# Attention output of four batches as one block of 64x64 matmul tiles in a fused attention and MoE kernel

## The chip, the cores and the metric

The kernel runs on one core of a Trainium2 chip. The metric is the device time of one execution in microseconds, as the median of several runs. The core has five engines that run side by side and wait for one another by semaphores: PE multiplies matrices into PSUM (eight banks), DVE and ACT do elementwise work and empty PSUM, POOL does elementwise work as well, and SP starts most of the DMA transfers.

## The reference

```python
def _attn_ref(q, k, v):                       # 8 batches, 8 heads, 576 rows, 64 columns
    q_s = softmax of q over its 64 columns
    k_s = softmax of k over the 576 rows
    kv  = einsum('bhsd,bhse->bhde', k_s, v)   # one 64x64 matrix per batch and head
    return einsum('bhsd,bhde->bhse', q_s, kv)

def _moe_ref(x, w_in, w_out, beta):           # x: 4608 x 512, the heads side by side
    h = x @ w_in                              # 512 -> 2048
    g = h * (1.0 / (1.0 + exp(-beta * h)))
    return g @ w_out                          # 2048 -> 512
```

(The two softmaxes are written out in the original; here they are shortened.) A batch has 576 rows: 512 make one slab, and the 64 remainder rows of all eight batches make a ninth.

## The kernel before

The program is a list of instructions recorded in order; each engine runs its own in that order, and a helper derives the semaphore waits from which buffers and PSUM banks each instruction reads and writes. The helper gives a PSUM bank one user at a time: an instruction that writes a bank waits until the other engines' earlier accesses to it are done.

Slab t (0 to 8) has a first part, x times `w_in` (64 matmuls of 512 columns), and a second part, g times `w_out`. The second part uses seven products in place of eight by sums and differences of blocks: seven products of 16 matmuls, 112 matmuls of 256 columns, in the fixed order below. PSUM banks `z5` and `z2` are used in turn.

```python
# second part of slab t (cut); one tick of the slot counter per matmul
prod_s(...); prod(z5, *gs2(0), *wo(1, 1), True, ...)   # matmuls 1 to 32
TS = PS[s];  TS = TS - PS[z5]                          # DVE
prod(z2, *gs2(1), *wo(0, 0), True)                     # 33 to 48
TS = TS - PS[z2]                                       # DVE: sets bank z2 free
if t > 3: g_diff(0); g_diff(1)                         # DVE
prod(z5, *gt(0, 0), *wo(0, 1), False); copy(z5, 0, 1, ACTE)    # 49 to 64
prod(z2, *gt(NG, 1), *wo(1, 0), False); copy(z2, 1, 0, ACTE)   # 65 to 80
prod(z5, *gt(0, 1), *wsum(1), False, True); last(z5, 1, 1)     # 81 to 96
prod(z2, *gt(NG, 0), *wsum(2), False, True); last(z2, 0, 0)    # 97 to 112
```

The attention of batch t+1 is placed between these matmuls at given slots (slot 64 is the start of the second part, and each of its matmuls counts 32/56). Two heads share a matmul whose 128x128 weights hold two 64x64 blocks and two blocks of masked zeros:

```python
def kvd(b, hp, bk, c):       # KVD = (K^T V) * 1/sum * MASK, 128x128 with zero corners
    ...
def out_mm(b, hp, bk):
    mm(PS[bk][:, :], KVD[kd(b)][:, hp, :], QT[i][:, hp, :], True, True, ...)
def out_step(b, hp, pool=MB, eng=DVE):     # one matmul and its copy out of PSUM
    ...
def attn(b):
    s = [(24 if b == 5 else 16, steps(kv_all, b))]
    x = []
    for hp in range(NHP):
        x += out_step(b, hp, MB, ACTE if hp % 2 else DVE)
    s += spread(x, 84, 108)
    return s
# and in slabs 4 to 6: eight remainder matmuls of 64 columns (outr_steps), spread too
```

The softmax here doesn't subtract the row's maximum and nothing guards it: scores larger than these inputs give would overflow.

Of the kernel before, what the change touches and what calls it, by code (L numbers as in the profile page):

```python
# [19 lines left out]
NM = DM // 128  # L20
NG = NF // 2
NHP = H // 2
SM = 512
SR = S - SM
NSLAB = 9
# [4 lines left out]


class Op:
    __slots__ = ("eng", "fn", "deps", "slot", "pos", "inc", "count", "clock")

    def __init__(self, eng, fn, slot):
        self.eng, self.fn, self.slot = eng, fn, slot
        self.deps = []
        self.inc = False
        self.count = 0
        self.clock = None  # L40


class Program:
# [46 lines left out]
    def plan(self):  # L90
        for op in self.ops:
            op.deps = [d for d in op.deps if not (d.eng == PE and op.eng == PE and d.slot is None)]
            for d in op.deps:
                d.inc = True
        counts = {}
        for op in self.ops:
            if op.slot is not None:
                key = ("dma", op.slot)
                counts[key] = counts.get(key, 0) + 16
                op.count = (key, counts[key])  # L100
            elif op.inc:
                key = ("eng", op.eng)
                counts[key] = counts.get(key, 0) + 1
                op.count = (key, counts[key])
        known = {}
        waits = []
        for op in self.ops:
            k = known.setdefault(op.eng, {})
            need = {}
            for d in sorted(op.deps, key=lambda d: -d.pos):  # L110
                key, n = d.count
                if k.get(key, 0) >= n:
                    continue
                if need.get(key, 0) < n:
                    need[key] = n
                for kk, nn in d.clock.items():
                    if k.get(kk, 0) < nn:
                        k[kk] = nn
                k[key] = max(k.get(key, 0), n)
            waits.append(sorted(need.items(), key=str))  # L120
            op.clock = dict(k)
            if op.count:
                op.clock[op.count[0]] = op.count[1]
        return counts, waits
# [31 lines left out]
def bass_efficient_attn_shen__then__act_swish_beta_kernel(  # L156
# [12 lines left out]
    with ExitStack() as es:  # L169
# [129 lines left out]
                load_rem("vrf", vt_h, VRF, b)  # L299


        def exp_main(name, srcb, dstb, b, hp0, n):
            i = b % 2
            for hp in range(hp0, hp0 + n):
                o = bass.AP(dstb[i], hp * 512, [[2048, 128], [64, 2], [128, 4], [1, 64]])
                a = bass.AP(srcb[i], hp * 512, [[2048, 128], [256, 2], [64, 4], [1, 64]])
                add(ACTE, lambda e, o=o, a=a: e.activation(o, a, ACT.Exp),  # L307
                    r=[(name + "f", i, hp)], w=[("e" + name, i, hp)])

# [14 lines left out]
                bass.AP(EKS[b], 0, [[512, 128], [1, 512]]), bass.AP(KRF, 0, [[512, 128], [1, 512]]),  # L324
                ACT.Exp), r=[("krf", 0), ("krf", 1)], w=[EKSK[b]])

        def exp_qr():
            add(ACTE, lambda e: e.activation(EQR[:, :, :], QRF[:, :, :], ACT.Exp),
                r=[("qrf", 0), ("qrf", 1)], w=["eqr"])

        def norm_main(b, hp0, n, eng=DVE, sums=True, mult=True):
            i = b % 2
# [21 lines left out]
        def cast_v(b, hp, eng=POOL, after=()):  # L354
            i = b % 2
            o = bass.AP(VB[i], hp * VW, [[4 * NHP * VW, 128], [NHP * VW, 4], [HW, 2], [1, 64]])
            a = bass.AP(VF[i], hp * 512, [[2048, 128], [64, 4], [256, 2], [1, 64]])
            add(eng, lambda e: (e.copy if eng == ACTE else e.tensor_copy)(o, a),  # L358
                r=[("vf", i, hp), ("vone", i)], w=[("vb", i, hp)], after=after)

# [63 lines left out]
        def kd(b):  # L424
            return b if b < 2 else 2 + b % 4

        def tiled(b):
            return b > 3

        def kvd(b, hp, bk, c):  # L430
            i = b % 2
            a = bass.AP(PS[bk], c, [[512, 128], [0 if tiled(b) else HW, 2], [1, D]])
            add(DVE, lambda e: e.scalar_tensor_tensor(
                KVD[kd(b)][:, hp, :].rearrange("p (a b) -> p a b", b=D), a, RC[i][:, hp:hp + 1],
                MASK[:, :].rearrange("p (a b) -> p a b", b=D), ALU.mult, ALU.mult),
                r=[("ps", bk), ("rc", i, hp), "mask0", "mask1", "mask2"], w=[("kvd", kd(b), hp)],
                bank=[bk])

        def kv_steps(b, hps, pool=MB):
            i = b % 2  # L440
            st = {}

            def one(n, hp, j):
                if n == 0 and j == 0:
                    st["b"] = bank(pool)
                bk = st["b"]
                l, r_, ke, kv, ko = kv_rows(b, hp, j)
                if not tiled(b):
                    mm(PS[bk][:, 256 * n:256 * n + VW - 1], l, r_[:, 0:VW - 1], j == 0, j == 4,
                       r=ke + kv, w=[("ps", bk)], bk=bk)  # L450
                for h in range(2) if tiled(b) else ():
                    p = slice(64 * h, 64 * h + 64)
                    add(PE, lambda e, h=h, p=p: e.matmul(  # L453
                        PS[bk][p, 256 * n:256 * n + D + 1], l[:, p], r_[:, HW * h:HW * h + D + 1],
                        start=j == 0, stop=j == 4, tile_position=(0, 64 * h),
                        skip_group_check=True),
                        r=ke + kv, w=[("ps", bk)], bank=[bk])
                if n == len(hps) - 1 and j == 4:
                    c, k_ = hps[0], len(hps)
                    s_ = bass.AP(PS[bk], D, [[512, 128], [256, k_]])  # L460
                    add(DVE, lambda e: e.reciprocal(RC[i][:, c:c + k_], s_),
                        r=[("ps", bk)], w=[("rc", i, h2) for h2 in hps], bank=[bk])
                    for m, h2 in enumerate(hps):
                        kvd(b, h2, bk, 256 * m)
            return [lambda n=n, hp=hp, j=j: one(n, hp, j) for n, hp in enumerate(hps)
                    for j in range(5)]
# [17 lines left out]
        def outr_steps(b):  # L484
# [14 lines left out]
                        w=[("xt8", pi)], bank=[bk])  # L499
            return [lambda hp=hp, e_=e_: one(hp, e_) for hp in range(NHP) for e_ in range(2)]  # L500

        def turn(b, hp0, n):
            i = b % 2
            o = bass.AP(QT[i], hp0 * 512, [[2048, 128], [128, 4 * n], [1, 128]])
            a = bass.AP(EQ[i], hp0 * 512, [[2048, 128], [1, 512 * n]])
            add(SP, lambda e: e.dma_start_transpose(o, a),
                r=[("eq", i, hp) for hp in range(hp0, hp0 + n)],
                w=[("qt", i, hp) for hp in range(hp0, hp0 + n)], slot=f"tq{i}{hp0}")
# [21 lines left out]
            return kv_steps(b, (0, 1)) + kv_steps(b, (2, 3))  # L530

        def attn(b):
            s = [(24 if b == 5 else 16, steps(kv_all, b))]
            x = []
            for hp in range(NHP):
                x += out_step(b, hp, MB, ACTE if hp % 2 else DVE)
            s += spread(x, 84, 108)
            return s

        def attn_late(b):  # L540
            x = []
            for hp in range(NHP):
                x += out_step(b, hp, MB, ACTE if hp % 2 else DVE)
            if b < 4:
                s = spread(kv_steps(b, (0, 1)), 97, 101) + spread(kv_steps(b, (2, 3)), 101, 105)
                s += [(105, lambda: g_diff(1))]
                return s + spread(x[0:2], 117, 120)
            s = [(96, steps(kv_all, b)), (99, lambda: g_diff(1))]
            return s + spread(x, 107, 123)

        def spread(steps, lo, hi):
            return [(lo + (hi - lo) * k / len(steps), s) for k, s in enumerate(steps)]
# [310 lines left out]
        for t in range(NSLAB):  # L863
# [13 lines left out]
            elif t < 4:  # L877
                todo = attn_late(t + 1)
                if t > 1:
                    todo += [(1, steps(out_step, t, 2, MB, ACTE)), (2.5, steps(out_step, t, 3))]  # L880
                if t == 3:
                    todo += [(4, one(norm_turn, 4, 2))]
                if t == 1:
                    todo += [(1, steps(out_step, 1, 2, (3,), ACTE)),
                             (3, steps(kv_steps, 1, (3,), (7,))),
                             (6, steps(out_step, 1, 3, (7,), DVE)),
                             (6.1, one(w_sum, 2, 4, 4)), (6.2, one(w_diff, 0)),
                             (6.3, one(w_diff, 1))]
            elif t < 7:
                todo = attn(t + 1)  # L890
                if t > 3:
                    todo += spread(outr_steps(2 * t - 5), *((72, 88), (72, 88), (60, 76))[t - 4])
            elif t == 7:
                todo = spread(outr_steps(1), 32, 48)
            todo = sorted(todo, key=lambda x: -x[0])
# [90 lines left out]
            elif t == 3:  # L986
# [3 lines left out]
                on(3, g_diff, 0)  # L990
                on(4, norm_turn, 5, 0)
                on(5, norm_turn, 5, 2)
                on(4, exp_qr)
                on(5, exp_k, 5)
                on(5, norm_turn_rem)
                on(5, casts, 5)
# [8 lines left out]
                on(3, norm_turn, b, 0)  # L1005
                on(4, norm_turn, b, 2)
            if 3 < t < 7:
                on(0, exp_qr)
                on(5, norm_turn_rem)
            if t in (4, 5):  # L1010
                on(0, load_rem, "qrf", qt_h, QRF, (6, 0)[t - 4])
# [35 lines left out]
```

## Time and profile before

| | before |
|---|---|
| median | 273.45 us (273.27 to 273.69, 6 runs) |
| PE busy | 97% of the span |
| PE on the chain that ended last | 85% |
| DVE, ACT busy | 71%, 67% |

PE sets the end, so the question for any change is what PE does, and for what PE waits. The lines are shown and read in the prediction. In this document I compare slabs by one length, taken from PE's timeline: from the start of the first matmul of the second part (the one with `WSUM,GS`) to the same matmul one slab later. Two of the lines from which the lengths before are taken (columns: start in us, us, engine and line, operation, out<-in, shape, count):

```profile
174.19 1.04 PE L754 MATMUL PS<-WSUM,GS 128*128 128x256 bf16 x8
202.28 0.60 PE L754 MATMUL PS<-WSUM,GS 128*128 128x256 bf16 x4
```

So slab 5 is 202.28 - 174.19 = 28.09 us long. By the same reading slab 3 is 28.63, slab 4 27.99, slab 6 27.28 and slab 7, whose second part holds no attention, 26.04.

### The profile page before, as it was taken

What the parts mean: (1) busy time and instruction counts of PE and PEld (TensorE: products, weight loads), DVE (VectorE), ACT (ScalarE), POOL (GpSimd) and SP (SyncE); (2) the same over time, 40 slices, a digit from 0 to 9 for tenths busy, and PEclk for the clock granted to TensorE, in tenths of its full rate; (3) what the DMA queues carried; (4) which work ended last, traced back from release to release, by engine and by line L of the source; (5) the groups of instructions that cost most, each with busy time, mean ns of one, the idle gap of its engine ahead of it and who ended that gap; (6) DMA issues with size and microseconds to landing.
All of it is one profiled execution on the core that took longest, in us unless ns stands there. A gap on an engine that the chain in (4) does not pass through costs nothing.

```text
span 271.7 us, 4811 instructions
## 1 busy us (share of the span) xinstructions
PE 263.8 (97%) x1882; PEld 165.7 (61%) x1905; DVE 194.0 (71%) x416; ACT 181.0 (67%) x284; POOL 64.1 (24%) x80
## 2 busy tenths in 40 slices
PE   8899999999999999999999999999999999999994
PEld 3444444448844885478646865687458745874683
DVE  4964586887867799878786977787687548626762
ACT  4898558789287956897778847893883387018610
POOL 2790010006530089000910870037000100000000
PEclk9999999999999999999999999999999999999999
DMA  7999999989799129930499999203800130012005
GB/s 220 314 201 207 227 321 349 303 227 373 173 337 285 65 53 299 332 95 2 89 282 283 308 345 182 103 20 65 208 0 2 31 142 2 0 69 88 0 5 152
DMA packets 59366, 45.93 MB, mean 169 GB/s; under 512 B 28608, under 2 KB 58320, under 8 KB 58320
## 3 DMA queue, kind: packets, MB, share of 16 engines
q1 hardware_dynamic: 54480, 40.90, 53.4%
q0 software_dynamic: 4240, 4.19, 9.4%
q10 hardware_dynamic: 624, 0.53, 0.6%
q8 instruction: 15, 0.25, 0.4%
q14 instruction: 7, 0.06, 0.1%
HBM read 36.71 MB, written 9.44 MB: 170 GB/s over the span
## 4 chain that ended last, share of the span: by engine, by line
PE 85%; DVE 4%; DMA 4%; POOL 2%; SPq 2%; issue 2%; ACT 1%; POOLq 0%
PE PS L387 51%; PE PS L754 33%; DMA VF<-in_v_dram 2%; DMA QT<-EQ 1%; PE PS L453 1%; POOL VB L358 1%; SPq L275 1%; DVE QS L339 1%; SPq L287 1%; DVE EQ L343 1%; POOL EQ L343 1%; DVE VB L358 1%; ACT GT L654 1%; POOL VR L372 0%; DVE QI L341 0%
## 5 line engine op out<-in xcount | busy, mean ns | idle before, releaser
L387 PE MATMUL PS<-XT,WIN 128*128 128x512 bf16 x562 | 126.2, 379 | 1.1 <-issue 0.3
L654 ACT ACTIVATE GT<-PS,BETA 128x512 bf16<-128x512 f32 x144 | 95.1, 689 | 37.8 <-PE PS L387 37.5
L387 PEld LDWEIGHTS PS<-XT,WIN 128*128 128x128 bf16 x576 | 55.2, 98 | 64.4 <-DVE XT L479 0.6
L677 DVE TENSOR_SCALAR GT<-GT,RB 128x512 bf16<-128x512 bf16 x144 | 52.1, 382 | 36.5 <-ACT GT L654 35.6
L343 POOL TENSOR_TENSOR EQ<-EQ,QI 128x1024 bf16<-128x1024 bf16 (+1 forms) x13 | 25.6, 1967 | 46.9 <-DVE QI L341 46.3
L754 PE MATMUL PS<-WOUT,GT 128*128 128x256 bf16 x256 | 33.0, 273 | 0.1
L754 PE MATMUL PS<-WOUT,GS 128*128 128x256 bf16 x256 | 31.9, 273 | 0.2
L754 PE MATMUL PS<-WSUM,GT 128*128 128x256 bf16 x256 | 30.4, 273 | 0.5 <-DMA QT<-EQ 0.4
L754 PEld LDWEIGHTS PS<-WSUM,GT 128*128 128x128 bf16 x256 | 25.0, 98 | 3.8 <-issue 0.3
L754 PEld LDWEIGHTS PS<-WOUT,GT 128*128 128x128 bf16 x256 | 24.9, 98 | 3.5
L790 ACT COPY O2S<-PS 128x512 f32<-128x512 f32 (+1 forms) x17 | 9.4, 560 | 25.6 <-PE PS L754 24.2
L754 PEld LDWEIGHTS PS<-WOUT,GS 128*128 128x128 bf16 x256 | 24.1, 98 | 3.4
L307 ACT ACTIVATE EQ<-QF 128x512 bf16<-128x512 f32 x32 | 17.9, 620 | 7.3 <-DMA QF<-in_q_dram 7.2
L358 POOL CAST VB<-VF 128x512 bf16<-128x512 f32 x24 | 16.7, 694 | 23.0 <-DVE GS L713 14.1
L713 DVE TENSOR_TENSOR GS<-GT 128x512 bf16<-128x512 bf16 (+2 forms) x32 | 21.9, 685 | 0.0
L339 DVE TENSOR_REDUCE QS<-EQ 128x16 f32<-128x1024 bf16 (+1 forms) x20 | 19.8, 991 | 0.9 <-ACT EQ L307 0.9
L720 DVE TENSOR_TENSOR GT<-GT 128x2048 bf16<-128x2048 bf16 x16 | 20.1, 1281 | 0.0
L307 ACT ACTIVATE EK<-KF 128x512 bf16<-128x512 f32 x32 | 18.1, 620 | 0.1
L479 ACT CAST XT<-PS 128x512 bf16<-128x512 f32 x18 | 10.3, 581 | 10.7 <-PE PS L387 10.7
L802 DVE TENSOR_TENSOR O2S<-TS,PS 128x512 f32<-128x512 f32 (+1 forms) x17 | 10.7, 643 | 9.5 <-PE PS L754 9.5
L754 PE MATMUL PS<-WSUM,GS 128*128 128x256 bf16 x128 | 16.7, 273 | 0.0
L387 PE MATMUL PS<-WOUT,GT 128*128 128x512 bf16 x62 | 15.0, 379 | 0.1
(82 smaller groups left out, 225.5 us busy)
## 6 DMA issues: line engine op xcount, KB each, us to landing
out_dram<-O2S SPq DMA_DIRECT2D x8, 1024.0 KB, 5.4
QF<-in_q_dram SPq DMA_DIRECT2D x6, 1024.0 KB, 5.9
KF<-in_k_dram SPq DMA_DIRECT2D x6, 1024.0 KB, 8.5
VF<-in_v_dram SPq DMA_DIRECT2D x6, 1024.0 KB, 12.2
KF<-in_k_dram SPq DMA_DIRECT2D x8, 256.0 KB, 5.5
VF<-in_v_dram SPq DMA_DIRECT2D x8, 256.0 KB, 5.5
WOUT<-in_moe_w_out_dram POOLq DMA_DIRECT2D x4, 512.0 KB, 16.4
WIN<-in_moe_w_in_dram POOLq DMA_DIRECT2D x3, 512.0 KB, 9.0
```

The source lines that it names most:

```text
L307: add(ACTE, lambda e, o=o, a=a: e.activation(o, a, ACT.Exp), r=[(name + "f", i, hp)], w=[("e" + name, i, hp)])
L339: add(DVE, lambda e: e.tensor_reduce(s_, a, AX.X, ALU.add), r=ks, w=[("qs", i, hp0)])
L343: add(eng, lambda e: e.tensor_tensor(a, a, vb, ALU.mult), r=ks + [("qi", i, hp0)], w=ks)
L358: add(eng, lambda e: (e.copy if eng == ACTE else e.tensor_copy)(o, a), r=[("vf", i, hp), ("vone", i)], w=[("vb", i, hp)], after=after)
L387: add(PE, lambda e: e.matmul(o, l, r_, start=start, stop=stop), r=r, w=w, bank=[bk])
L479: add(eng, lambda e: (e.copy if eng == ACTE else e.tensor_copy)(XT[i][:, hp, :], PS[bk][:, :]), r=[("ps", bk)], w=[("xt", i, hp)], bank=[bk])
L654: add(ACTE, lambda e: e.activation(GT[:, f, :], PS[bk][:, :], ACT.Silu, scale=BETA[:, f:f + 1]), r=[("ps", bk), "beta"], w=[("gt", f, 0), ...
L677: add(DVE, lambda e: e.tensor_scalar(GT[:, f, :], GT[:, f, :], RB[:, f:f + 1], None, ALU.mult), r=k + ["rb"], w=k)
L713: add(DVE, lambda e: e.tensor_tensor(GS2[:, i:i + n, :], GT[:, i:i + n, :], GT[:, i + NG:i + NG + n, :], ALU.add), r=[k_ for f in (i, i + ...
L720: add(DVE, lambda e: e.tensor_tensor(gv(f, th, NG), gv(f, th, NG), gv(f, 1 - th, NG), ALU.subtract), r=gk(f, 0, NG) + gk(f, 1, NG), w=gk(f ...
L754: add(PE, lambda e, l=l, r_=r_, st=st, u=u, i=i, b_=b_: e.matmul(PS[b_][:, 256 * u:256 * u + 256], l, r_, start=st, stop=end and i == NG - ...
L802: add(DVE, lambda e, b_=b_, u0=u0, u1=u1: e.tensor_tensor(o[:, u0:u1, :], ts[:, u0:u1, :], bank3(b_)[:, u0:u1, :], ALU.add), r=["ts", ("ps ...
```

## The change

The 64x64 blocks of two heads fill only half of a 128x128 weight matrix; the rest is zeros. The change splits the array into four 64x64 tiles: for batches 4 to 7 all outputs of a batch are made by eight small matmuls in one block, and of the three remainder groups of slabs 4 to 6, two join the blocks of batches 6 and 7. Heads are paired (0,2), (1,3), (4,6), (5,7), so that each result lands in the right rows. These batches no longer need the mask.

```diff
+PAIRS = ((0, 2), (1, 3), (4, 6), (5, 7))
...
+        def kvd_t(b, c, n, bk):        # two pairs of heads at once, no mask
+            ...
+        def quad(b, pi=None):
+            bks = list(MB) + [HB[(hrot[0] + 1) % 3], HB[(hrot[0] + 2) % 3]]
+            b_r = bks[4]
+            def x_mm(g, a):            # two 64x64 tiles of row group a
+                rows = slice(64 * a, 64 * a + 64)
+                for c in range(2):
+                    hp, bk = 2 * g + c, bks[2 * g + a]
+                    ... matmul(PS[bk][64 * c:64 * c + 64, :], KVD[kd(b)][rows, hp, 0:D],
+                        QT[i][rows, hp, :], ..., tile_position=(64 * a, 64 * c))
+            def r_mm(a):               # eight remainder tiles of row group a, all in bank b_r
+                ...                    # the second half waits for the first (op.hard)
+            x_mm(0, 1)
+            r_mm(0)
+            x_mm(0, 0)
+            x_mm(1, 1)
+            x_mm(1, 0)
+            r_mm(1)
+            for x in (1, 0, 3, 2):     # copies: 1 and 3 on ACT, 0 and 2 on DVE
+                ...
+            if pi is not None:         # remainder: one copy, on DVE
+                add(DVE, lambda e: e.tensor_copy(o, a), r=[("ps", b_r)], w=[("xt8", pi)], ...)
...
         def attn(b):
-            s = [(24 if b == 5 else 16, steps(kv_all, b))]
-            x = []
-            for hp in range(NHP):
-                x += out_step(b, hp, MB, ACTE if hp % 2 else DVE)
-            s += spread(x, 84, 108)
-            return s
+            return [(24 if b == 5 else 16, steps(kv_all, b)),
+                    (90, one(quad, b, b - 4 if b > 5 else None))]
...
-                if t > 3:
-                    todo += spread(outr_steps(2 * t - 5), *((72, 88), (72, 88), (60, 76))[t - 4])
+                if t == 4:
+                    todo += spread(outr_steps(3), 72, 88)
```

(Cut to its core; the paired reads in the exp and cast helpers, the exp of the remainder in two halves, and batch 4's block at slot 112 in slab 3 are left out.)

More of the change, by code (lines that the diff above doesn't have):

```diff
@@ L32 @@
 class Op:
-    __slots__ = ("eng", "fn", "deps", "slot", "pos", "inc", "count", "clock")
+    __slots__ = ("eng", "fn", "deps", "slot", "pos", "inc", "count", "clock", "hard")
     def __init__(self, eng, fn, slot):
@@ L37, in __init__ @@
         self.deps = []
+        self.hard = ()
         self.inc = False
@@ L92, in plan @@
             op.deps = [d for d in op.deps if not (d.eng == PE and op.eng == PE and d.slot is None)]
+            op.deps.extend(op.hard)
             for d in op.deps:
@@ L299, in load, with tiled, pair @@
                 load_rem("vrf", vt_h, VRF, b)
+        def tiled(b):
+            return b > 3
+        def pair(b, hp):
+            if tiled(b):
+                return PAIRS[hp][0], PAIRS[hp][1] - PAIRS[hp][0]
+            return 2 * hp, 1
         def exp_main(name, srcb, dstb, b, hp0, n):
@@ L305, in exp_main @@
                 o = bass.AP(dstb[i], hp * 512, [[2048, 128], [64, 2], [128, 4], [1, 64]])
-                a = bass.AP(srcb[i], hp * 512, [[2048, 128], [256, 2], [64, 4], [1, 64]])
+                h0, dh = pair(b, hp)
+                a = bass.AP(srcb[i], h0 * 256, [[2048, 128], [dh * 256, 2], [64, 4], [1, 64]])
                 add(ACTE, lambda e, o=o, a=a: e.activation(o, a, ACT.Exp),
@@ L325, in exp_kr_s, with exp_qr @@
                 ACT.Exp), r=[("krf", 0), ("krf", 1)], w=[EKSK[b]])
-        def exp_qr():
-            add(ACTE, lambda e: e.activation(EQR[:, :, :], QRF[:, :, :], ACT.Exp),
-                r=[("qrf", 0), ("qrf", 1)], w=["eqr"])
+        def exp_qr(pi):
+            for g in range(2) if tiled(2 * pi) else (None,):
+                if g is None:
+                    o, a = (bass.AP(x, 0, [[512, 128], [1, 512]]) for x in (EQR, QRF))
+                else:
+                    o = bass.AP(EQR, 256 * g, [[512, 128], [128, 2], [64, 2], [1, 64]])
+                    a = bass.AP(QRF, 256 * g, [[512, 128], [64, 2], [128, 2], [1, 64]])
+                add(ACTE, lambda e, o=o, a=a: e.activation(o, a, ACT.Exp),
+                    r=[("qrf", 0), ("qrf", 1)], w=["eqr"])
         def norm_main(b, hp0, n, eng=DVE, sums=True, mult=True):
@@ L356, in cast_v @@
             o = bass.AP(VB[i], hp * VW, [[4 * NHP * VW, 128], [NHP * VW, 4], [HW, 2], [1, 64]])
-            a = bass.AP(VF[i], hp * 512, [[2048, 128], [64, 4], [256, 2], [1, 64]])
+            h0, dh = pair(b, hp)
+            a = bass.AP(VF[i], h0 * 256, [[2048, 128], [64, 4], [dh * 256, 2], [1, 64]])
             add(eng, lambda e: (e.copy if eng == ACTE else e.tensor_copy)(o, a),
@@ L425, in kd @@
             return b if b < 2 else 2 + b % 4
-        def tiled(b):
-            return b > 3
         def kvd(b, hp, bk, c):
             i = b % 2
-            a = bass.AP(PS[bk], c, [[512, 128], [0 if tiled(b) else HW, 2], [1, D]])
+            a = bass.AP(PS[bk], c, [[512, 128], [HW, 2], [1, D]])
             add(DVE, lambda e: e.scalar_tensor_tensor(
@@ L437, in kvd @@
                 bank=[bk])
+        def kvd_t(b, c, n, bk):
+            i = b % 2
+            a = bass.AP(PS[bk], 0, [[512, 128], [256, n], [1, D]])
+            rc = bass.AP(RC[i], c, [[NHP, 128], [1, n], [0, D]])
+            add(DVE, lambda e: e.tensor_tensor(KVD[kd(b)][:, c:c + n, 0:D], a, rc, ALU.mult),
+                r=[("ps", bk)] + [("rc", i, h2) for h2 in range(c, c + n)],
+                w=[("kvd", kd(b), h2) for h2 in range(c, c + n)], bank=[bk])
         def kv_steps(b, hps, pool=MB):
@@ L452, in one @@
                     p = slice(64 * h, 64 * h + 64)
-                    add(PE, lambda e, h=h, p=p: e.matmul(
-                        PS[bk][p, 256 * n:256 * n + D + 1], l[:, p], r_[:, HW * h:HW * h + D + 1],
+                    lh, rh = l[:, p], r_[:, HW * h:HW * h + D + 1]
+                    if j == 4:
+                        g = PAIRS[hp][h]
+                        lh = EKR[(b // 2) % 2][:, g, :]
+                        rh = VR[(b // 2) % 2][i][:, g // 2, HW * (g % 2):HW * (g % 2) + D + 1]
+                    add(PE, lambda e, h=h, p=p, lh=lh, rh=rh: e.matmul(
+                        PS[bk][p, 256 * n:256 * n + D + 1], lh, rh,
                         start=j == 0, stop=j == 4, tile_position=(0, 64 * h),
@@ L462, in one @@
                         r=[("ps", bk)], w=[("rc", i, h2) for h2 in hps], bank=[bk])
+                    if tiled(b):
+                        kvd_t(b, c, k_, bk)
+                        return
                     for m, h2 in enumerate(hps):
@@ L500, in outr_steps @@
             return [lambda hp=hp, e_=e_: one(hp, e_) for hp in range(NHP) for e_ in range(2)]
+        def quad(b, pi=None):
+            i = b % 2
+            bks = list(MB) + [HB[(hrot[0] + 1) % 3], HB[(hrot[0] + 2) % 3]]
[4 more added lines that the diff above has]
+                    hp, bk = 2 * g + c, bks[2 * g + a]
+                    add(PE, lambda e, c=c, hp=hp, bk=bk: e.matmul(
+                        PS[bk][64 * c:64 * c + 64, :], KVD[kd(b)][rows, hp, 0:D],
+                        QT[i][rows, hp, :], start=True, stop=True,
+                        tile_position=(64 * a, 64 * c), skip_group_check=True),
+                        r=[("kvd", kd(b), hp), ("qt", i, hp)], w=[("ps", bk)], bank=[bk])
+            def r_mm(a):
+                rows = slice(64 * a, 64 * a + 64)
+                for g, e_, c in ([(g, e_, c) for g in range(2) for e_ in range(2)
+                                  for c in range(2)] if pi is not None else ()):
+                    hp, d, o = 2 * g + c, kd(2 * pi + e_), 256 * a + 128 * g + 64 * e_
+                    op = add(PE, lambda e, c=c, hp=hp, d=d, o=o, e_=e_: e.matmul(
+                        PS[b_r][64 * c:64 * c + 64, o:o + 64], KVD[d][rows, hp, 0:D],
+                        QTR[rows, hp, 64 * e_:64 * e_ + 64], start=True, stop=True,
+                        tile_position=(64 * a, 64 * c), skip_group_check=True),
+                        r=[("kvd", d, hp), "qtr"], w=[("ps", b_r)], bank=[b_r])
+                    if not done or done[0][0] == a:
+                        done[:] = done[-1:] + [(a, op)]
+                    else:
+                        op.hard = [o_ for a_, o_ in done if a_ != a]
+            done = []
+            x_mm(0, 1)
[5 more added lines that the diff above has]
+            for x in (1, 0, 3, 2):
+                eng, bk = (DVE, ACTE)[x % 2], bks[x]
+                add(eng, lambda e, eng=eng, x=x, bk=bk: (
+                    e.copy if eng == ACTE else e.tensor_copy)(XT[i][:, x, :], PS[bk][:, :]),
+                    r=[("ps", bk)], w=[("xt", i, x)], bank=[bk])
+            if pi is not None:
+                o = bass.AP(XT8, pi * 128, [[NM * SM, 128], [SM, 2], [2 * SM, 2], [1, 128]])
+                a = bass.AP(PS[b_r], 0, [[512, 128], [256, 2], [128, 2], [1, 128]])
+                add(DVE, lambda e: e.tensor_copy(o, a), r=[("ps", b_r)], w=[("xt8", pi)],
+                    bank=[b_r])
@@ L532, in attn @@
         def attn(b):
-            s = [(24 if b == 5 else 16, steps(kv_all, b))]
-            x = []
-            for hp in range(NHP):
-                x += out_step(b, hp, MB, ACTE if hp % 2 else DVE)
-            s += spread(x, 84, 108)
-            return s
+            return [(24 if b == 5 else 16, steps(kv_all, b)),
+                    (90, one(quad, b, b - 4 if b > 5 else None))]
         def attn_late(b):
-            x = []
-            for hp in range(NHP):
-                x += out_step(b, hp, MB, ACTE if hp % 2 else DVE)
             if b < 4:
+                x = []
+                for hp in range(2):
+                    x += out_step(b, hp, MB, ACTE if hp % 2 else DVE)
                 s = spread(kv_steps(b, (0, 1)), 97, 101) + spread(kv_steps(b, (2, 3)), 101, 105)
                 s += [(105, lambda: g_diff(1))]
-                return s + spread(x[0:2], 117, 120)
+                return s + spread(x, 117, 120)
             s = [(96, steps(kv_all, b)), (99, lambda: g_diff(1))]
-            return s + spread(x, 107, 123)
+            return s + [(112, one(quad, b))]
         def spread(steps, lo, hi):
@@ L992, in bass_efficient_attn_shen__then__act_swish_beta_kernel @@
                 on(5, norm_turn, 5, 2)
-                on(4, exp_qr)
+                on(4, exp_qr, 1)
                 on(5, exp_k, 5)
@@ L1007, in bass_efficient_attn_shen__then__act_swish_beta_kernel @@
             if 3 < t < 7:
-                on(0, exp_qr)
+                on(0, exp_qr, (2, 3, 0)[t - 4])
                 on(5, norm_turn_rem)
```

## The prediction

> **What bounds the kernel now.** I read the busy times and the chain that ended last, then the table of stretches and the timelines of the slabs in which the change acts. There are nine slabs, 0 to 8; each has a first part (64 matmuls of 512 columns) and a second (112 of 256 columns). Attention for batch t+1 is squeezed into slab t, so batches 4 to 7 lie in slabs 3 to 6.
>
> ```profile
> PE 263.8 (97%) x1882; PEld 165.7 (61%) x1905; DVE 194.0 (71%) x416; ACT 181.0 (67%) x284; POOL 64.1 (24%) x80
> ...
> PE 85%; DVE 4%; DMA 4%; POOL 2%; SPq 2%; issue 2%; ACT 1%; POOLq 0%
> ```
>
> PE is on 85% of the chain, and in slabs 3 to 6 on nearly all of it. So PE time taken out there shortens the kernel, unless PE then waits. The second part of slab 5, as stretches of the chain (start, us, what):
>
> ```profile
> 179.06 0.76 PE PS L754 x7
> 179.83 0.22 PE PS L387
> 180.04 1.20 PE PS L754 x11
> ```
>
> The 0.22 us piece is one of the four attention-output matmuls (128x512) of the batch, laid between layer matmuls at 0.109 us each; a remainder matmul (64 columns) takes 0.03 us in the same view. What attention costs on PE in all is read from the stretches of the second part: slabs 4, 5, 6, then slab 7, which has none there (stretch, length, busy times):
>
> ```profile
> 146.20:159.70 13.50, 13.43 (x124) 11.68 (x125) 11.32 (x19) 10.71 (x18) 7.97 (x8) 1.00 1.11 296
> 174.19:187.73 13.54, 13.44 (x124) 11.68 (x125) 11.37 (x20) 10.20 (x17) 5.28 (x6) 1.00 0.09 21
> 202.28:215.73 13.45, 13.35 (x123) 11.60 (x123) 9.10 (x17) 6.13 (x8) 1.04 (x1) 1.00 0.05 11
> 229.72:241.95 12.23, 12.23 (x113) 10.91 (x112) 6.32 (x11) 1.86 (x3) 0.00 (x0) 1.00 0.00 1
> ```
>
> Against slab 7's 12.23 us, slabs 4 and 5 spend 1.27 and 1.31 us on 4 outputs and 8 remainder matmuls (4 x 0.22 + 8 x 0.03 = 1.12, the rest small waits). Slab 6 spends 1.22 us, and 3 of its remainder matmuls lie before the stretch, about 0.1 us more.
>
> **What the Trainium skill says.** "TensorEngine Tiling (Array Packing)", Key Properties, says that changing the tiling mode drains the array. The kernel before already changes mode for the K^T V matmuls of batches 4 to 7 (two column tiles), so this trace has the price:
>
> ```profile
> 123.03 0.93 PE L754 MATMUL PS<-WOUT,GT 128*128 128x256 bf16 x7
> 123.89 0.32 PE L453 MATMUL PS<-VB,EK 128*64 128x65 bf16 x8
> ...
> 124.51 0.20 PE L453 MATMUL PS<-VR,EKR 128*64 128x65 bf16 x2
> 124.64 0.61 PE L754 MATMUL PS<-WOUT,GT 128*128 128x256 bf16 x4
> ```
>
> Seven layer matmuls at 0.109 us from 123.03 would let the next start at 123.80; it starts at 123.89, so 0.09 to go in. The 40 tiled ones start 0.016 us apart, so the last has been started by 124.53 and the next is due at 124.55; the layer resumes at 124.64, so 0.09 to come out. It agrees: about 0.2 us per round trip. "TensorE: Matmul & The Clock Gate", Part 3, says that tiles of different row and column groups run at once. The trace shows it for columns (65 columns at 0.016 us each, against 0.03 us for 64 untiled); for rows nothing here shows it yet. The tiling page's Restrictions and Gotchas, Gotcha 1, says that different row tiles may not use one PSUM bank at once; the change obeys it with separate banks for the outputs and one wait of PE on itself between the two halves of the remainder. The same page, Performance Considerations, PSUM Bottleneck, says that tiling speeds up TensorE but not the emptying of PSUM. That becomes my main doubt.
>
> **The change, part by part.** (1) Each batch's four 128x512 matmuls, half of whose weights are masked zeros, become eight 64x64-tile matmuls of 512 columns, four at a time: two rounds. (2) The remainder of batches 4 and 5 moves from slab 5's early second part into the block of batch 6, and that of batches 6 and 7 into the block of batch 7: sixteen 64x64 tiles of 64 columns, eight per row group. The remainder of batches 2 and 3 stays spread in slab 4, that of 0 and 1 in slab 7. (3) The outputs were spread over slots 84 to 108; they now come at once after the 46th matmul of the second part (slabs 4 to 6), or after the 84th (slab 3). (4) The masked KVD scaling, 4 instructions of 0.347 us a batch, becomes 2 unmasked ones. (5) The remainder exp becomes two halves, and heads are paired (0,2), (1,3) and so on; the reads keep shape and size. Parts 4 and 5 touch DVE and ACT, off the chain here; I count nothing for them.
>
> PE cost of a block, an estimate from the durations above: two rounds, the row groups staggered, 2 x 0.22 + 0.03 = 0.47, plus 0.2 for the mode, is 0.67 us. With the remainder, row group 0 does its eight (8 x 0.016 = 0.13) while row group 1 does its first outputs, and the other way round at the end: 0.6 + 0.2 = 0.80 us. Before: 0.88 without and 1.12 with remainder. Gross gain: slabs 3 and 4 0.21 each, slabs 5 and 6 0.32 each, 1.06 in all; with the small waits of the spread form (0.15 to 0.2 per slab) perhaps 1.4.
>
> **What comes back as a wait.** DVE in slab 5, before:
>
> ```profile
> 178.97 0.68 DVE L479 CAST XT<-PS 128x512 bf16<-128x512 f32 x1
> 179.57 0.68 DVE L498 CAST XT<-PS 128x512 bf16<-128x512 f32 x1
> 180.30 0.69 DVE L832 TENSOR_TENSOR TS<-TS,PS 128x512 f32<-128x512 f32 x1
> 180.90 2.35 DVE L720 TENSOR_TENSOR GT<-GT 128x2048 bf16<-128x2048 bf16 x2
> ```
>
> The L832 subtraction frees the bank that the 65th matmul writes; before, it ended at 180.9 and that matmul started at 182.06 (181.30 plus 7 x 0.109 in PE's timeline), 1.1 us of slack. The order of the changed program puts three copies out of PSUM (two XT, then XT8) ahead of it, 0.60 us apart, all of which wait for the block. Count from the block's start Q: first copy's bank ready at Q+0.6 (0.16 for the remainder, 0.22 of streaming, 0.2 latency), copies done Q+2.4, subtraction done Q+3.0. PE reaches the 65th at Q + 0.70 (block without the way in) + 18 x 0.109 = Q+2.66. So PE waits about 0.4 us in slabs 5 and 6. In slab 4 the XT8 copy comes earlier, so two copies precede the subtraction and nothing waits there; but the block's first DVE bank is the one XT8 must leave, about 0.1 us. In slab 3 the copies stand behind DVE's sums at the slab's end, and slab 4 needs the first at once; some 0.25 us of slack, so perhaps a small wait.
>
> Sum against the stretches: slab 3 about -0.2; slab 4 from 13.50 to 12.23 + 0.24 + 0.67 + 0.1 = 13.24, -0.25; slab 5 from 13.54 to 12.23 + 0.80 + 0.4 = 13.43, -0.1; slab 6 the same 13.43 with its 0.1 outside, about -0.1. Together some -0.6, less about 0.1 for slab 3's end: 273.48 - 0.5 = 273.0 us.
>
> **The rivals.** (a) No new wait: DVE's copies run faster or the subtraction isn't reached late. Then the full 1.0 to 1.4 comes through: about 272.2. Against it stand 0.60 us between copies and a slack of only 1.1 us. (b) The four tiles don't run at once, only two columns of them: a block is four rounds, 0.9 + 0.2, longer than what it replaces, and the waits grow with it: about 274.2. The skill's page is against it, no row of this trace decides it. (c) ACT: in slab 4 the exps end at 153.7, then two copies and the z5 copy, due by 155.4, and PE needs it near 155.9. Slack 0.4 us, so no wait; were it one, +0.3. (d) The wait of PE on itself or the weight loads of the small tiles stretch the block by 0.2 in two slabs: +0.4.
>
> **Range and chances.** The gain is a fraction of a per cent whichever way: the whole PE work touched is 4 us of 273 (1.5%), so neither side of 2% can be reached by it. I take (main theory) six in ten, (a) two in ten, (b) or (d) two in ten: range 272.2 to 273.9. Faster by over 2%: 0.01; within 2%: 0.98; slower by over 2%: 0.01.
>
> **What would show it.** Right: 64x512 output matmuls starting in quads, so that a block without remainder takes 0.6 to 0.7 us; the stretch of slab 5 at 13.3 to 13.5, with PE waiting 0.3 to 0.5 us for the L832 subtraction ahead of the 65th matmul, in slabs 5 and 6 and not in slab 4. Wrong: that wait missing (a); row tiles starting 0.2 us after one another (b); PE waiting for ACT's copy instead (c).

## The result, and the profile after

The changed kernel takes 273.92 us (median of 6 runs, 273.69 to 274.29) against 273.45 us in the same rounds. The ratio is 1.0017, with a 95% interval of 1.0004 to 1.003. (Ratios are the mean time of one kernel's fast runs over that of the other's of the same rounds, so not quite the ratio of the medians.) So the change is a little slower: inside 2%, just outside the predicted range, and on the other side of zero from the predicted gain.

The page after, busy times of the engines and their shares of the chain:

```profile
PE 264.3 (97%) x1918; PEld 164.7 (61%) x1937; DVE 192.4 (71%) x408; ACT 181.1 (67%) x286; POOL 62.1 (23%) x80
...
PE 88%; DVE 5%; DMA 2%; SPq 2%; issue 1%; ACT 0%
```

DVE does less work than before (194.0 to 192.4 us) but has a larger share of the chain (4% to 5%). The chain in slab 5 after (start, us, what) shows where:

```profile
178.85 0.15 PE PS L543
179.00 0.10 PE PS L554 x7
179.10 0.43 PE PS L543 x6
179.53 0.30 PE PS L554 x8
179.83 0.34 PE PS L830 x2
180.17 0.66 DVE XT L573
180.83 0.60 DVE XT L579
181.43 0.60 DVE TS L908
182.03 0.05 issue
182.08 5.42 PE PS L830 x48
```

L543 are the outputs, L554 the remainder, L830 the layer; an edit shifts these line numbers, so the same instruction has a slightly different one in other runs. "issue" is time in which the engine waited for nothing that the profile shows. After the block the chain leaves PE for three DVE instructions, two copies and the subtraction L908, before PE goes on with the last 48 matmuls. Before, the chain stayed on PE through all of this. PE's timeline of the same stretch (columns as above; in brackets the idle time just before and what ended it):

```profile
178.78 0.40 PE L543 MATMUL PS<-QT,KVD 64*64 64x512 bf16 x2
178.78 0.31 PE L554 MATMUL PS<-QTR,KVD 64*64 64x64 bf16 x8
178.93 0.60 PE L543 MATMUL PS<-QT,KVD 64*64 64x512 bf16 x6
179.52 0.31 PE L554 MATMUL PS<-QTR,KVD 64*64 64x64 bf16 x8
179.76 0.39 PE L830 MATMUL PS<-WOUT,GS 128*128 128x256 bf16 x2
179.99 1.91 PE L830 MATMUL PS<-WOUT,GT 128*128 128x256 bf16 x16
182.08 1.92 PE L830 MATMUL PS<-WOUT,GT 128*128 128x256 bf16 x16 [0.18 <-DVE TS L908]
```

And DVE's timeline, the three copies and the subtraction:

```profile
179.54 1.29 DVE L573 CAST XT<-PS 128x512 bf16<-128x512 f32 x2 [1.13 <-PE PS L543]
180.75 0.68 DVE L579 CAST XT<-PS 128x512 bf16<-128x512 f32 x1
181.34 0.68 DVE L908 TENSOR_TENSOR TS<-TS,PS 128x512 f32<-128x512 f32 x1
```

The reader is to see three things. The 65th matmul was due at 179.99 + 16 x 0.109 = 181.74 and starts at 182.08, so PE loses 0.34 us to the subtraction (the bracket shows only 0.18, because the 16 matmuls before it are shown as busy for 1.91 us, 0.16 longer than 16 x 0.109). The subtraction ends at 182.02 because it stands behind three copies, which wait for the block: the two outputs at 179.54, then the remainder. And the second half of the remainder starts only at 179.52, 0.43 us after the first half ended (178.78 + 0.31). The six outputs in between take part of that; the rest is PE's wait for itself, 0.29 us as two_banks shows below.

Slab 5 is now bounded by these lines, 202.00 - 173.66 = 28.34 us:

```profile
173.66 1.47 PE L830 MATMUL PS<-WSUM,GS 128*128 128x256 bf16 x12
202.00 1.25 PE L830 MATMUL PS<-WSUM,GS 128*128 128x256 bf16 x10
```

| length, us | slab 3 | slab 4 | slab 5 | slab 6 | slab 7 | sum |
|---|---|---|---|---|---|---|
| before | 28.63 | 27.99 | 28.09 | 27.28 | 26.04 | 138.03 |
| after | 28.42 | 27.95 | 28.34 | 27.71 | 26.04 | 138.46 |
| difference | -0.21 | -0.04 | +0.25 | +0.43 | 0 | +0.43 |

The sum, +0.43 us, fits the medians (+0.47). The spans of the two profiled runs do not show it (271.7 us both), because slab 1, where the two kernels run the same instructions, was 0.27 us shorter in the profiled run of the changed kernel. Below, that slab turns out to be the noisy one.

### The profile page after: what moved, and what is told of

The parts are those of the page before. It is cut to its first block, busy times and chain, and to the rows that moved or that the text cites. A ratio compares the mean times of both kernels' runs of the same rounds, so it can differ in the third digit from the quotient of the medians.

```text
span 271.7 us, 4870 instructions
## 1 busy us (share of the span) xinstructions
PE 264.3 (97%) x1918; PEld 164.7 (61%) x1937; DVE 192.4 (71%) x408; ACT 181.1 (67%) x286; POOL 62.1 (23%) x80
## 4 chain that ended last, share of the span: by engine, by line
PE 88%; DVE 5%; DMA 2%; SPq 2%; issue 1%; ACT 0%
PE PS L406 51%; PE PS L830 35%; DMA VF<-in_v_dram 2%; PE PS L482 1%; PE PS L543 1%; DVE QS L357 1%; SPq L278 1%; SPq L290 1%; DVE EQ L361 1%; DVE XT L573 1%; DVE VB L377 1%; DVE TS L908 0%; DVE XT L579 0%; DVE QI L359 0%; DVE XT L511 0%
## 5 line engine op out<-in xcount | busy, mean ns | idle before, releaser
L753 DVE TENSOR_SCALAR GT<-GT,RB 128x512 bf16<-128x512 bf16 x144 | 53.3, 392 | 36.3 <-ACT GT L730 35.5
L830 PE MATMUL PS<-WOUT,GT 128*128 128x256 bf16 x256 | 32.2, 273 | 0.4 <-DVE TS L908 0.4
L830 PE MATMUL PS<-WOUT,GS 128*128 128x256 bf16 x256 | 31.3, 273 | 0.0
L830 PE MATMUL PS<-WSUM,GT 128*128 128x256 bf16 x256 | 30.1, 273 | 0.3 <-DMA QT<-EQ 0.2
L830 PEld LDWEIGHTS PS<-WSUM,GT 128*128 128x128 bf16 x256 | 24.8, 98 | 3.9 <-issue 0.9
L830 PEld LDWEIGHTS PS<-WOUT,GT 128*128 128x128 bf16 x256 | 24.7, 98 | 3.6 <-DVE TS L908 0.9
L830 PEld LDWEIGHTS PS<-WOUT,GS 128*128 128x128 bf16 x256 | 24.3, 98 | 3.3 <-issue 0.4
L377 POOL CAST VB<-VF 128x512 bf16<-128x512 f32 x24 | 14.8, 616 | 21.9 <-DVE GS L789 13.2
L830 PE MATMUL PS<-WSUM,GS 128*128 128x256 bf16 x128 | 16.6, 273 | 0.0
L784 DVE TENSOR_TENSOR GS<-GT 128x256 bf16<-128x256 bf16 (+2 forms) x32 | 13.6, 426 | 1.1
```

What stands on the lines that cost most here:

```text
L377: add(eng, lambda e: (e.copy if eng == ACTE else e.tensor_copy)(o, a), r=[("vf", i, hp), ("vone", i)], w=[("vb", i, hp)], after=after)
L753: add(DVE, lambda e: e.tensor_scalar(GT[:, f, :], GT[:, f, :], RB[:, f:f + 1], None, ALU.mult), r=k + ["rb"], w=k)
L784: add(DVE, lambda e: e.tensor_tensor(GS1[:, i:i + n, :], gv(i, 0, n), gv(i + NG, 1, n), ALU.add), r=gk(i, 0, n) + gk(i + NG, 1, n), w=[("g ...
L830: add(PE, lambda e, l=l, r_=r_, st=st, u=u, i=i, b_=b_: e.matmul(PS[b_][:, 256 * u:256 * u + 256], l, r_, start=st, stop=end and i == NG - ...
```

## The experiments

Two theories stood after this comparison. Theory A: the loss is PE's wait for the subtraction behind DVE's queue of copies. Theory B: the loss is PE's wait on itself inside the block. Both are seen in the trace; which of them counts, this trace alone does not tell, since one can hide behind the other.

**sub_first.** The block of slabs 5 and 6 comes three matmuls later, so that the subtraction is recorded ahead of the copies.

```diff
-                    (90, one(quad, b, b - 4 if b > 5 else None))]
+                    (91.8 if b > 5 else 90, one(quad, b, b - 4 if b > 5 else None))]
```

> The block of slabs 5 and 6 comes three matmuls later (after the 49th), so that DVE's subtraction that frees the bank of the 65th matmul stands before the three copies instead of behind them; nothing else is changed. Theory A (the loss is PE waiting for that subtraction behind the queue of copies): the wait ahead of the 65th matmul (0.34 us in each of slabs 5 and 6) is gone, the second parts of the two slabs get 0.3 shorter each, time about 273.3, 0.6 below the change. Theory B (the loss is PE's wait on itself between the two halves of the remainder, 0.29 us a block): that wait stays, the time stays within 0.2 of the change, 273.9.

Measured: slab 5 27.98 and slab 6 27.36 us, 0.36 and 0.35 shorter than in the change; all other slabs from 3 on as before to 0.01 us. DVE's timeline in slab 5 has the order that was meant, the subtraction first and the copies 4.3 us later:

```profile
179.18 0.69 DVE L908 TENSOR_TENSOR TS<-TS,PS 128x512 f32<-128x512 f32 x1 [0.70 <-PE PS L830]
...
183.47 1.22 DVE L573 CAST XT<-PS 128x512 bf16<-128x512 f32 x2
184.60 0.68 DVE L579 CAST XT<-PS 128x512 bf16<-128x512 f32 x1
```

The median was 273.64 us (273.14 to 273.81, 5 runs), 0.3 rather than the expected 0.6 below the change; its ratio to the kernel before is 1.0006 (0.9993 to 1.002). The slabs' lengths say theory A; the medians alone would have left it open.

**two_banks.** The second half of the remainder gets the bank that the first product has left, so PE need not wait for itself; two copies of 256 columns take the place of one of 512.

```diff
-            b_r = bks[4]
+            b_r = (bks[4], HB[hrot[0] % 3])
...
-                    if not done or done[0][0] == a: ...
-                    else: op.hard = [o_ for a_, o_ in done if a_ != a]
```

> The second half of the remainder goes into a bank of its own (the one that the first product of the slab has left), so PE no longer waits on itself; DVE empties the two halves by two copies of 256 columns in place of one of 512. Theory A: the block gets 0.3 us shorter (0.8 from the last layer matmul before it to the next after it), but the copies start no earlier and are 0.15 longer in all, so PE only waits longer for the subtraction, 0.6 to 0.8 us, and the time stays at 273.9 to 274.2. Theory B: the time falls by 0.5 to 0.6, to 273.4.

Measured: 274.27 us (274.04 to 274.48, 5 runs), slab 5 28.40 and slab 6 27.77 us, even 0.06 longer than in the change. The block did get shorter, from 1.08 to 0.79 us (from where the next layer matmul was due to where it starts), but PE only stands longer at the 65th matmul; its timeline in slab 5:

```profile
180.18 1.91 PE L827 MATMUL PS<-WOUT,GT 128*128 128x256 bf16 x16
182.63 1.05 PE L827 MATMUL PS<-WOUT,GT 128*128 128x256 bf16 x8 [0.54 <-DVE TS L905]
```

Due at 180.18 + 16 x 0.109 = 181.92, started at 182.63: a wait of 0.71 us. Theory B alone is refuted: 0.29 us taken from the block bought nothing, as long as the copies set the pace.

**xt8_act.** The remainder's copy goes from DVE to ACT.

```diff
-                add(DVE, lambda e: e.tensor_copy(o, a), r=[("ps", b_r)], w=[("xt8", pi)],
+                add(ACTE, lambda e: e.copy(o, a), r=[("ps", b_r)], w=[("xt8", pi)],
```

> The remainder's copy out of PSUM in slabs 5 and 6 goes to ACT instead of DVE, so two copies and not three precede the subtraction. Theory A: the subtraction ends 0.6 us earlier, the wait of 0.34 us is gone in both slabs, about 273.3; ACT has slack, so its later copy (due before the 81st matmul) does not hold PE up. Theory B: no change, 273.9.

Measured: 273.19 us (272.75 to 273.33, 5 runs), ratio 0.9986 (0.9974 to 0.9999); slabs 5 and 6 27.99 and 27.36 us, the same as with the subtraction first, by another way. In slab 5 DVE's subtraction now starts right behind two copies, and PE's 32 matmuls run through without a wait at the 65th:

```profile
181.13 0.68 DVE L908 TENSOR_TENSOR TS<-TS,PS 128x512 f32<-128x512 f32 x1
180.37 3.66 PE L830 MATMUL PS<-WOUT,GT 128*128 128x256 bf16 x32
```

Two independent ways of getting the subtraction from behind a copy take away the same 0.35 us per slab. Theory A holds.

**no_rem.** The blocks of slabs 5 and 6 do without the remainder; POOL sets its part of slab 8's input to zero. The result is wrong (relative error 0.24).

```diff
-            r_mm(0)
-            r_mm(1)
-                add(DVE, lambda e: e.tensor_copy(o, a), r=[("ps", b_r)], w=[("xt8", pi)], ...)
+                add(POOL, lambda e: e.memset(o, 0.0), w=[("xt8", pi)])
```

> Wrong on purpose: the blocks of slabs 5 and 6 do without the remainder of batches 4 to 7 (its part of the input of slab 8 is set to zero by POOL), so neither the self-wait nor the third copy is there. Both theories: block of 0.65 to 0.7 us as in slab 3, no wait ahead of the 65th matmul; 1.4 to 0.7 us or 0.7 less per slab, time 272.5. It shows whether the first DVE copy starts 0.6 us after the block's start when no remainder stands before it (in the change it was 0.76).

Measured: 272.48 us (272.23 to 273.03, 5 runs), slabs 5 and 6 27.56 and 26.94 us, 0.78 and 0.77 shorter than in the change. The block takes 0.65 us as in slab 3, and no wait follows. The first DVE copy starts 0.49 us after the block's start, not 0.76; the block on PE's timeline of slab 5:

```profile
179.53 0.63 PE L543 MATMUL PS<-QT,KVD 64*64 64x512 bf16 x8
```

and on DVE's:

```profile
180.02 1.29 DVE L571 CAST XT<-PS 128x512 bf16<-128x512 f32 x2 [0.86 <-PE PS L543]
```

This run also showed why the profiled runs scatter (that the other runs behind the medians scatter for the same reason is likely, not shown). Slab 1, with the same instructions in all these kernels, was 29.53 us long here, 28.30 in the change, 28.57 before and 29.00 with the remainder's copy on ACT. The view of who waits for whom (us in total, times, longest) has PE waiting for the transposing DMA; in this run:

```profile
PE PS L406 <- DMA QT<-EQ: 1.1, 1, 1.1
```

and in the changed kernel:

```profile
PE PS L830 <- DMA QT<-EQ: 0.2, 1, 0.2
```

The slower of the slab's two transposes landed 3.2 us after its issue in the change, 3.5 before, 4.0 with the remainder's copy on ACT and 4.5 here: the order of the slab's lengths.

**change_again.** The changed kernel, unaltered, beside the next two.

> The changed kernel once more, unaltered, on the same chip and in the same rounds as the next two, because single-slab effects of 0.3 us are as large as the run-to-run scatter: 273.9 +- 0.3, and the lengths from the second part of slab 3 on as before to 0.05 us (28.42, 27.95, 28.34, 27.71, 26.04).

Measured: 273.90 us (273.76 to 274.60, 5 runs) against 273.71 for the kernel before, ratio 1.0015 (1.0003 to 1.0027); lengths 28.42, 27.96, 28.34, 27.71, 26.04. The small loss repeats (0.19 us between the medians here, 0.47 in the first comparison), and the lengths repeat to 0.01 us.

**both.** The subtraction first and the second bank together (the two edits above).

> Subtraction first (the block of slabs 5 and 6 after the 49th matmul) and the second half of the remainder in its own bank, together. Theory A, under which the self-wait is hidden only while the queue of copies decides: now it pays, slab 5 27.69 and slab 6 27.07 (0.65 less than the change in each), time 1.2 to 1.3 us below the change, 272.6, and 0.8 below the kernel before. If the self-wait cost nothing at all, it would equal the run with the subtraction first alone (27.98 and 27.36).

Measured: 272.81 us (272.51 to 273.04, 5 runs), ratio 0.9968 (0.9956 to 0.998); slabs 5 and 6 27.69 and 27.06 us. The second bank, worth nothing alone, is worth 0.29 to 0.30 us per slab here, because PE's own work is what sets the pace again. So the self-wait was real but hidden.

**both_all.** Slab 4's block too comes after the 49th matmul.

```diff
-                    (91.8 if b > 5 else 90, one(quad, b, b - 4 if b > 5 else None))]
+                    (91.8, one(quad, b, b - 4 if b > 5 else None))]
```

> As the one before, and slab 4's block too comes after the 49th matmul, so that the bank that the earlier remainder copy holds is free when the block starts: slab 4 gets 0.05 to 0.1 shorter than 27.95, all else as in both; time 272.5.

Measured: 272.42 us (271.90 to 273.10, 6 runs), ratio 0.9958 (0.9944 to 0.9971). Slab 4 is 27.79 us, 0.16 shorter, more than expected; its block takes 0.65 us now, and took 0.82 in the change, where one bank was still being emptied of the earlier remainder. This version beats both kernels: 1.3 us below the kernel before (273.71) and 1.5 below the change in the same rounds; by the lengths of slabs 3 to 7, which leave slab 1 out, it is 1.03 below the kernel before (137.00 against 138.03).

**rows_apart.** Only the order in the block: the outputs of row group 0 first, then those of row group 1.

```diff
-            x_mm(0, 1)
-            r_mm(0)
-            x_mm(0, 0)
-            x_mm(1, 1)
-            x_mm(1, 0)
+            x_mm(0, 0)
+            x_mm(1, 0)
+            r_mm(0)
+            x_mm(0, 1)
+            x_mm(1, 1)
             r_mm(1)
```

> Only the order inside the block is changed: the four outputs of row group 0 first, then the four of row group 1, so that the row groups no longer take turns. If the four tiles really run at once in the change (block of slab 3: 0.65 us between the layer matmuls around it, beyond their own time), two rounds become three to four and the block of slab 3 grows by 0.2 to 0.25, to 0.87 or 0.9. If row groups run one after another anyway, it stays 0.65.

Measured (one execution, state unknown, but slabs 3 and 7 are as long as in the fast runs): the block of slab 3 takes 0.65 us, as in the change, so the expected growth did not come. My expectation was badly built, since its other branch was no better: if a 512-column matmul on a tile takes 0.216 us, as in the layer, eight fit into 0.65 us only if more than two run at once on average (8 x 0.216 = 1.73, and 1.73 / 0.65 = 2.7), whatever their order. A row group has two tiles, so by this estimate both row groups work at once, in either order; what PE's records of single starts mean in a tiled block stays open. The time (274.15 us) tells nothing. Slabs 5 and 6 got 0.14 shorter (28.20 and 27.57 us): the bank of the first DVE copy is now written first, so that copy starts 0.45 us after the block's start and the subtraction ends 2.93 us after it. The block with the remainder got longer, from 1.08 to 1.30 us (why is open), so PE comes to the 65th matmul only 3.17 us after the block's start, and its wait of 0.34 us there is gone. Slab 4 got 0.11 longer (28.06 us), since the bank that is now written first is the one that the earlier remainder copy still holds:

```profile
151.87 0.63 PE L543 MATMUL PS<-QT,KVD 64*64 64x512 bf16 x8 [0.19 <-DVE XT L530]
```

**rem_last.** With two banks, the whole remainder after all outputs.

```diff
-            r_mm(0)
             x_mm(0, 0)
             x_mm(1, 1)
             x_mm(1, 0)
+            r_mm(0)
             r_mm(1)
```

> The kernel with a second bank for the remainder, and in the block all outputs first, both halves of the remainder after them. It asks why the first DVE copy starts 0.76 us after the block's start in slabs 5 and 6, with or without the wait of PE on itself, where I had counted 0.6, and 0.49 without a remainder. If the remainder matmuls ahead of that copy's outputs cause all of it, the copy starts at 0.49 here, the subtraction ends 0.27 earlier, and the length of slab 5 goes from 28.40 (two banks) to 28.13 (wait of 0.54 down to about 0.2). If something else in the block with remainder delays it, it stays at 0.76 and 28.4.

Measured (one execution, 273.51 us, state unknown, slabs 3 and 7 as in the fast runs): slab 5 28.12 us, and the first copy starts 0.49 us after the block's start. Block and wait on PE's timeline of slab 5:

```profile
178.95 0.63 PE L543 MATMUL PS<-QT,KVD 64*64 64x512 bf16 x8
179.41 0.32 PE L554 MATMUL PS<-QTR,KVD 64*64 64x64 bf16 x16
...
182.04 1.70 PE L827 MATMUL PS<-WOUT,GT 128*128 128x256 bf16 x14 [0.23 <-DVE TS L905]
```

and the first copies on DVE's:

```profile
179.44 1.29 DVE L569 CAST XT<-PS 128x512 bf16<-128x512 f32 x2 [0.86 <-PE PS L543]
```

As expected: the eight remainder matmuls ahead of the first copied outputs delay the whole queue of copies by 0.27 us, though they start 0.016 us apart, which would make 0.13. Where the other 0.14 comes from is open.

## Why the prediction was wrong

The mechanism was right and the sum was not. Point by point:

- **The block's own cost was right where nothing disturbed it.** 0.67 us was predicted for a block without remainder; slab 3 has 0.65 and gained 0.21, against "about -0.2". That fits the price of the mode change that the kernel before had shown. With the remainder 0.80 was predicted; 1.08 was measured, and 0.79 once the self-wait was gone. So rival (d) came true inside the block, at 0.29 us, but cost the change nothing, as two_banks shows.
- **The wait for the subtraction was right in kind and place**: slabs 5 and 6, not slab 4, 0.34 us against 0.4. But PE came to it 0.30 us later than I said (at Q+2.96, not Q+2.66, for the self-wait), so the right size of the wait is luck: it hides an error in when the subtraction ends. I had counted Q+3.0; it ended at 182.02 with the block's start Q at 178.78, so at Q+3.24. The failed step is "first copy's bank ready at Q+0.6 (0.16 for the remainder ...)": the copy started at Q+0.76, and rem_last and no_rem show that the remainder ahead of it costs 0.27, and without it the copy starts at Q+0.49 where 0.22 + 0.2 = 0.42 had been counted. The rest is the subtraction's own last piece (0.68 rather than the 0.60 spacing). That is 0.24 us in each of the two slabs.
- **The failed step with the larger share is the baseline of the stretches**: "Against slab 7's 12.23 us, slabs 4 and 5 spend 1.27 and 1.31 us". I had taken slab 7's stretch from the chain, which dates a piece from the end of the one before, and the starts of the others from PE's timeline, and these differ. The chain's piece:

```profile
229.72 12.23 PE PS L754 x112
```

In PE's timeline of the kernel before, slab 7's second part runs from 229.56 to the next recorded matmul of the first part at 242.00, 12.44 us:

```profile
229.56 0.82 PE L754 MATMUL PS<-WSUM,GS 128*128 128x256 bf16 x6
...
240.80 1.15 PE L754 MATMUL PS<-WSUM,GT 128*128 128x256 bf16 x9
242.00 0.59 PE L387 MATMUL PS<-XT,WIN 128*128 128x512 bf16 x2
```

- The difference of 0.21 is one matmul: the last of the second part starts at 240.80 + 8 x 0.109 = 241.67, so the next is due at 241.78; that record is most likely missing (the profile has 562 records of these matmuls and 576 of their weight loads), and the first recorded one comes 0.22 later. The same gap stands at the ends of the stretches of slabs 4, 5 and 6, so these hold one first-part matmul more than the chain's 12.23, which is just the 112 matmuls (112 x 0.109 = 12.21). Against 12.44, slabs 4 and 5 spent 1.06 and 1.10 us, close to the 4 x 0.22 + 8 x 0.03 = 1.12 of the terms. "The rest small waits" and "with the small waits of the spread form (0.15 to 0.2 per slab) perhaps 1.4" were a fault of the reading. Corrected by 0.21, the predicted stretches give -0.05 for slab 4 (measured -0.04), +0.1 for slab 5 and +0.2 for slab 6; with the late subtraction +0.34 and +0.43. Slab 6 measured +0.43. Slab 5 measured +0.25, since its length also holds three remainder matmuls (0.09) that the change took out of slab 6's first part. So these two steps, 0.63 us for the baseline in three slabs and 0.48 for the subtraction in two, account for the difference to within a few hundredths.
- **Slab 3's end**: the "about 0.1 us" that I set aside for it did not come; slab 3 gained its full 0.21.
- **Slab 4**: the bank held by the earlier remainder was named at about 0.1; both_all shows 0.16. That -0.05 and -0.04 agree so well is in part luck: the stretch's end, 159.70, is no start in PE's timeline, which has 159.74, and the 0.04 cancels most of this 0.06.
- **Small readings** on which nothing rests: the block of slab 3 comes after the 85th matmul, not the 84th, and the L832 subtraction ended at 180.99 (180.30 + 0.69), not 180.9.
- **Rivals.** (a), no new wait, failed as the change stands; its gross gain without the small waits, 1.06 us, is close to the 1.03 by which the slabs of both_all are shorter than before, in which the waits are taken away. (b), rows one after the other, is refuted by the 0.65 us block (0.9 + 0.2 was forecast for it). (c), ACT holding PE, did not come, not even with a third copy on ACT.

## What to carry to other kernels

When matmuls are packed into one quick block, the copies that empty PSUM also come in one burst, so look at which instruction stands behind the burst on the copying engine, and who waits for it; here moving the block by three matmuls was worth 0.35 us a slab, more than the 0.21 us that the tiles themselves gained in slab 3. Place what frees a bank first and the copies that nobody needs soon behind it. And take the length of a stage by one and the same event in one view at both ends, since a lost record (0.22 us) is as large as the effects that matter here.

## What the Trainium skill lacked or had wrong

- "TensorEngine Tiling (Array Packing)", Key Properties, says that a mode change drains the array but gives no price. Here it was about 0.09 us in and 0.09 us out, for two column tiles as read in the prediction, and the 0.65 us block of 64x64 tiles fits the same price, if it is two rounds (an estimate: 0.65 - 2 x 0.216 = 0.22).
- The same page, Gotcha 1, says that software must keep two row tiles from one bank, but not what that costs: the wait of PE on itself made the block 1.08 instead of 0.79 us, and a second bank removed it.
- The tiling page's PSUM Bottleneck advises using both DVE and ACT to empty PSUM. The change did, and lost all the same; the page does not say that what stands behind the copies counts: 0.34 us of wait per slab, gone in either of two runs.
- No page gives how much a transposing DMA scatters between runs: in the profiled runs of kernels with the same instructions there, the slower transpose of slab 1 landed 3.2 to 4.5 us after its issue, and the slab was 28.30 to 29.53 us long.
